# An attention and two-MLP kernel that pins every engine's instruction order with its own list schedule

## Chip, cores and metric

One core of a Trainium2 chip. The metric is device microseconds of one execution, the median of several runs. The profile is of one execution; times in it count from the span's start.

## What is computed

```python
# attention: batch 4, heads 8, seq 576, head_dim 64; f is a forget gate
scores = scale * (q @ k^T) + cum[:, :, :, None] - cum[:, :, None, :]   # cum = cumsum(log(clip(f)))
scores = where(causal, -1e9, scores)
x = softmax(scores) @ v                     # reshaped to 2304 tokens x 512
# first MLP, d_ff 2048
h = x @ w_in
g = h * tanh(softplus(h))
x = g @ w_out
# second MLP, d_ff 1024
h = x @ w_in2
solu = h * softmax(h)
ln = (solu - mean) / sqrt(var + 1e-6) * g_ln
out = ln @ w_out2
```

The weights of the MLPs arrive as 64-bit floats; every product is made of three products of 16-bit halves (high and low).

## The kernel before

The kernel is one stream of instructions that `emit` writes in program order. A scheduler of the framework then sets each engine's order by its own estimate of when operands are there; the kernel adds order edges by hand (`later`) in a few places. Engines run in order and wait on semaphores.

**Head.** SP loads k, q, v in chunks of 128 rows. `split_k`, `split_q`, `split_v` scale a chunk and split it into halves (`split`, L198 to L206: a cast on ScalarE, a subtraction on VectorE or GpSimd); DMA transposes bring k and q into place (L376, L398). The first MLP's weights come in 16 parts of 1 MB (`wi_r0` to `wi_r7`, `wo_r0` to `wo_r7`, two buffers), loaded at L124. `Weight.conv` turns a part into 32-bit floats with three VectorE instructions (L137, L139, L141) and squares it on TensorE into a Gram matrix (L160); after every second part `Weight.bound` finds a scale and `Weight.split` splits the two parts.

**Attention.** For each batch b, row block i (0 to 4) and group of heads: scores on TensorE (L436 to L441), maximum on VectorE (L483, L496), exponential on ScalarE (L485, L499, L500), high half by one of three engines (L519 GpSimd, L521 VectorE, L523 ScalarE), low half by GpSimd (L524), a DMA transpose (L529), and three pv-matmuls per chunk (L555 to L557). `fin` scales the result (L570 to L574) and transposes it into `xT`.

**First MLP.** 9 blocks of 256 tokens, 16 column tiles each. `up` makes a tile of h with 12 matmuls (L785). For two tiles at a time, `mish_a` and `mish_b` compute the activation (ScalarE L797 to L805, VectorE's clamp L802 on `ta` and its product L806 on `th`), `mish_c` casts and subtracts (ScalarE L811, GpSimd L812), and `down` adds the tile into the block's outputs (L829, 12 matmuls for two tiles and each half). Block 0 is accumulated in four parts on VectorE (L838, L840). `evac` scales the block's rows (L851 to L871) and stores them.

**Second MLP.** Its weights (`w2i_r0` to 3, `w2o_r0` to 3) are loaded when attention's memory is released, converted and scaled in the same way (squares on ScalarE, L150; row scale L147; sum over partitions on TensorE, L984). `first` computes 24 matmuls per token tile into h2 (L1028), the normalised z on VectorE, ScalarE and GpSimd (L1035 to L1056), and transposes it; `second` does the last 24 matmuls (L1068).

Program order interleaves these: `att_slots` says how many attention steps go ahead of each half tile of the first MLP, `wgo` how many weight steps.

Of the kernel before, what the change touches and what calls it, by code (L numbers as in the profile page):

```python
# [2 lines left out]

# [19 lines left out]
DFF, DFF2 = 2048, 1024  # L23
NC1 = DM // P
# [62 lines left out]
def later(tc, a, b):

    tc.add_manual_dep(
        getattr(a, "ins", a), getattr(b, "ins", b).name,  # L90
        mybir.DependencyInfo(mybir.DependencyClass.NoSync, mybir.DependencyReason.DATA),
        reason="issue order")
# [9 lines left out]
class Weight:  # L102

    last = None

    def __init__(self, tc, pool, nm, dst, slots, src, across, group=None, row_scale=None, after=None, gram=None):
        self.across = across  # L110
        self.tc, self.nc, self.pool, self.nm, self.dst, self.n = tc, tc.nc, pool, nm, dst, slots // 2
        self.src, self.row_scale = src, row_scale
        self.group, self.after, self.gram = (group or slots) // 2, after, gram
        self.f64 = src(0).dtype != F32
        self.f32 = dst.rearrange("p s e -> p (s e)").bitcast(F32).rearrange("p (s e) -> p s e", e=512)
        if gram is None:
            self.stat = pool.tile([P, self.n], F32, name=f"{nm}_stat")
        self.raw, self.scale, self.slot = {}, {}, {}
        self.bounds = pool.tile([P, self.n // self.group, 8], F32, name=f"{nm}_b")

    def load(self, n):
        src = self.src(n)
        t = self.pool.tile([P, 2, 512], src.dtype, tag="w64", name=f"{self.nm}_r{n}", bufs=WB)
        i = self.nc.sync.dma_start(t, src)  # L124
        if self.after is not None and self.after():
            later(self.tc, i, self.after())
        self.raw[n] = t
        return i

    def conv(self, n):  # L130
        nc = self.nc
        raw = self.raw.pop(n)
        f = self.f32[:, 2 * n + 2:2 * n + 4]
        if self.f64:
# [18 lines left out]
        g, r = divmod(n, self.group)  # L153
        if r == 0:
            self.slot[g] = self.gram.pop(0)
            self.gram.append(self.slot[g])
        o = self.slot[g]
        w = f.bitcast(BF16).rearrange("p s (c e t) -> p (s c) e t", c=4, t=2)[:, :, :, 1]
        for c in range(8):
            i = nc.tensor.matmul(  # L160
                o, w[:, c], w[:, c], start=(r == 0 and c == 0), stop=(r == self.group - 1 and c == 7))
            if c == 0 and Weight.last is not None:
                later(self.tc, i, Weight.last)
            Weight.last = i
# [44 lines left out]
def emit(tc, q, k, v, f, w_in, w_out, w2_in, w2_out, g_ln, out):  # L209
    nc = tc.nc  # L210
# [10 lines left out]
        out=maskd, in_=maskd, pattern=[[-1, P]], compare_op=ALU.is_ge,  # L221
# [19 lines left out]
    win = const.tile([P, NC1 * DFF // 512 + 2, 1024], F16, name="win")  # L241
# [17 lines left out]
    ft = rp0.tile([B * H, S], F32, name="ft")  # L259
    nc.sync.dma_start(ft, f.rearrange("b h s -> (b h) s"))  # L260
    nc.vector.tensor_scalar(ft, ft, 1e-4, 1.0, op0=ALU.max, op1=ALU.min)
    lf = rp0.tile([B * H, S], F32, name="lf")
    first_ln = nc.scalar.activation(lf, ft, AF.Ln)
    with tc.issue_after(getattr(first_ln, "ins", first_ln)):
        nc.scalar.preload_act_table_set("natural_log_exp_and_others")
    nc.vector.memset(ft, 1.0)
    dt_ = rp0.tile([B * H, S], F32, name="dt_")
    nc.vector.tensor_tensor_scan(dt_, ft, lf, 0.0, op0=ALU.mult, op1=ALU.subtract)
# [19 lines left out]
    kt, vt, qt = {}, {}, {}  # L288
# [102 lines left out]
    def split_q(b, c):  # L391
        r0, r1_, t0 = rows_of(b, c)
        t = attd.tile([P, H, P], F16, tag="qn", name=f"qn_{b}_{c}", bufs=1)
        rq = hd(raw["q", b, c][r0:r1_])
        s = sc["q", b][r0:r1_]
        split(nc, t[r0:r1_, :, :64], t[r0:r1_, :, 64:], rq, s, qmode(b, c, 2))
        qa = attd.tile([P, H, P], F16, tag="qa", name=f"qa_{b}_{c}", bufs=2)
        pend["qt"] = nc.sync.dma_start_transpose(out=qa[:, :, r0:r1_], in_=t[r0:r1_].rearrange("p h d -> p (h d)"))  # L398
        qb_ = qb[cnt["qb"] % 2]
        cnt["qb"] += 1  # L400
        nc.vector.tensor_copy(qb_[:64, :, r0:r1_], qa[:64, :, r0:r1_])  # L401
        qt[b, c] = (qa, qb_)

    pend = {}
# [97 lines left out]
    def step_h(b, i, hs):  # L502
        m, pt = pend.pop(("p", b, i, hs))
        n = len(hs) * (i + 1)
# [20 lines left out]
        if n == i + 1 and o == 0:  # L525
            pend["ph", b, i] = ph
            return
        pT = attd.tile([P, 4 * NCH, P], F16, tag="pT", name=f"pT_{b}_{i}_{h0}", bufs=PTB)
        pend["pt"] = nc.sync.dma_start_transpose(  # L529
            out=pT[:, :2 * (o + n), :m], in_=ph[:m, :2 * (o + n)].rearrange("p c s -> p (c s)"))  # L530
        pend["pT", b, i, h0] = pT

# [26 lines left out]
    def fin(b, i):  # L559
# [168 lines left out]
    def pool0(c):  # L728
        return spare if c < 3 else None
# [390 lines left out]
```

## Time and profile before

| | |
|---|---|
| three runs, us | 857.27, 857.79, 859.59 (median 857.79) |
| span of the profiled execution, us | 856.0 |
| TensorE busy | 739.0 us (86%) |
| VectorE busy | 617.6 us (72%) |
| ScalarE busy | 548.2 us (64%) |
| GpSimd busy | 440.8 us (51%) |
| mean granted TensorE clock | 0.977 |
| HBM read, written | 46.59 MB, 9.55 MB |

Which execution was profiled is not among the numbers, so its own time is its span plus what lies outside it; the median of the runs is 1.8 us above the span. Busy time counts an instruction from start to end, so it holds the time in which an instruction has begun and waits inside. Matmuls overlap, and a busy TensorE is not one at its full pace.

### The profile page before, as it was taken

To read this page: it belongs to the slowest core of one execution; us is meant where nothing else is said; L and a number is where in the kernel's file an instruction comes from. 1 tells how busy PE (TensorE), PEld (TensorE's weight loads), DVE (VectorE), ACT (ScalarE), POOL (GpSimd) and SP (SyncE) were. 2 spreads that over 40 slices of the span, in tenths; PEclk is the share of its full clock that TensorE was granted. 3 is DMA by queue.
4 is the path that set the end of the run, shared out by engine and by line. 5 is a ranking of instruction groups with operands and counts; after the bars stand their busy time and mean duration, and the time that the engine had idled before them with its cause. 6 is when DMAs were issued, how large, how long until landed. Compare 5 with 4: busy or idle time off the path is not lost.

```text
span 856.0 us, 15746 instructions
## 1 busy us (share of the span) xinstructions
PE 739.0 (86%) x5822; PEld 456.4 (53%) x5822; DVE 617.6 (72%) x1158; ACT 548.2 (64%) x1202; POOL 440.8 (51%) x341
## 2 busy tenths in 40 slices
PE   0545776689999999997999999986999999999998
PEld 0334543447656666575666767553555554444443
DVE  6799999498867989769896755599566444665551
ACT  5645647868779877877877767686855554333331
POOL 2268676755976667755678653128832222022110
PEclk9999997889999999999999999999999999999999
DMA  9999555477899898988897533941013323344443
GB/s 239 229 215 281 160 176 94 93 137 145 153 174 190 168 169 153 184 155 153 173 180 119 115 70 63 233 156 61 26 38 87 74 64 73 87 101 106 104 88 82
DMA packets 328568, 114.83 MB, mean 134 GB/s; under 512 B 317676, under 2 KB 317676, under 8 KB 328492
## 3 DMA queue, kind: packets, MB, share of 16 engines
q1 hardware_dynamic: 328492, 113.84, 63.9%
q8 instruction: 45, 0.74, 0.4%
q14 instruction: 31, 0.25, 0.1%
HBM read 46.59 MB, written 9.55 MB: 66 GB/s over the span
## 4 chain that ended last, share of the span: by engine, by line
PE 37%; DVE 24%; DMA 12%; ACT 11%; issue 8%; POOL 6%; SPq 1%; DVEq 0%; ACTq 0%; POOLq 0%
PE h L1028 11%; PE o L1068 10%; PE x L829 7%; PE h L785 6%; DMA pT<-ph 3%; POOL ph L524 3%; DVE th L806 2%; DVE ta L802 2%; ACT p L485 2%; DVE ph L521 1%; DMA w2i_r<-in_moe_w_in_dram 1%; DMA ktr<-kn 1%; DMA rawk<-in_k_dram 1%; ACT p L500 1%; DVE nm L483 1%
## 5 line engine op out<-in xcount | busy, mean ns | idle before, releaser
L829 PE MATMUL x<-wout,gt 128*128 128x512 f16 x864 | 219.8, 387 | 18.2 <-ACT gt L811 8.8
L785 PE MATMUL h<-xT,win 128*128 128x256 f16 x1728 | 221.2, 277 | 2.3 <-POOL win L203 1.7
L524 POOL TENSOR_TENSOR ph<-p,ph 128x512 f16<-128x512 f32 (+4 forms) x120 | 157.0, 1314 | 81.3 <-ACT ph L523 35.0
L785 PEld LDWEIGHTS <-win 128*128 128x128 f16 x1728 | 168.5, 100 | 45.8 <-POOL win L203 1.8
L812 POOL TENSOR_TENSOR gt<-th,gt 128x512 f16<-128x512 f32 x72 | 92.4, 1284 | 106.5 <-ACT gt L811 105.3
L829 PEld LDWEIGHTS <-gt 128*128 128x128 f16 x864 | 80.0, 100 | 99.3 <-ACT gt L811 11.6
L1056 POOL TENSOR_TENSOR z<-sl,z 128x1024 f16<-128x1024 f32 x18 | 38.7, 2151 | 138.0 <-DVE s2c L1035 111.1
L1028 PE MATMUL h<-w,x2T 128*128 128x512 f16 x432 | 98.4, 380 | 2.9 <-POOL w L206 1.6
L1068 PE MATMUL o<-wo,zT 128*128 128x512 f16 x432 | 96.5, 379 | 0.5 <-DMA zT<-z 0.5
L555 PE MATMUL pv<-vt,pT 128*128 128x64 f16 (+3 forms) x480 | 71.4, 203 | 23.0 <-DMA pT<-ph 20.2
L806 DVE SCALAR_TENSOR_TENSOR th<-ta,th 128x512 f32<-128x512 f32 x72 | 71.9, 1000 | 24.7 <-ACT ta L805 24.4
L485 ACT ACTIVATE p<-sp,nm 64x64 f32<-64x64 f32 (+7 forms) x128 | 61.3, 484 | 38.7 <-DVE nm L483 21.1
L436 PE MATMUL sp<-ktr,qa 128*128 128x64 f16 (+6 forms) x304 | 59.6, 253 | 22.8 <-ACT p L485 8.7
L811 ACT CAST gt<-th 128x512 f16<-128x512 f32 x72 | 44.3, 615 | 50.2 <-DVE th L806 49.9
L802 DVE TENSOR_SCALAR ta<-ta 128x512 f32<-128x512 f32 x72 | 58.8, 816 | 20.4 <-ACT ta L797 19.9
L1028 PEld LDWEIGHTS <-x2T 128*128 128x128 f16 x432 | 42.3, 98 | 53.9 <-issue 4.0
L555 PEld LDWEIGHTS <-pT 128*128 128x128 f16 (+3 forms) x480 | 45.4, 101 | 47.9 <-DMA pT<-ph 31.3
L556 PE MATMUL pv<-vt,pT 128*128 128x64 f16 (+3 forms) x480 | 70.4, 198 | 0.6 <-DVE vt L199 0.6
L557 PE MATMUL pv<-vt,pT 128*128 128x64 f16 (+3 forms) x480 | 70.2, 198 | 0.0
L1068 PEld LDWEIGHTS <-zT 128*128 128x128 f16 x432 | 42.2, 98 | 51.5 <-DMA zT<-z 1.0
L437 PE MATMUL sp<-ktr,qb 67*128 67x64 f16 (+6 forms) x304 | 63.3, 254 | 3.6 <-DVE qb L401 3.6
L1039 ACT ACTIVATE e<-h,s2c 128x1024 f32<-128x1024 f32 x18 | 21.7, 1204 | 68.1 <-DVE s2c L1037 68.1
(235 smaller groups left out, 1443.5 us busy)
## 6 DMA issues: line engine op xcount, KB each, us to landing
wi_r<-in_moe_w_in_dram SPq DMA_DIRECT2D x8, 1024.0 KB
wo_r<-in_moe_w_out_dram SPq DMA_DIRECT2D x8, 1024.0 KB
rawk<-in_k_dram SPq DMA_DIRECT2D x25, 256.0 KB
rawv<-in_v_dram SPq DMA_DIRECT2D x25, 256.0 KB
x2d<-x2h SPq DMA_DIRECT2D x18, 256.0 KB
out_dram<-ro SPq DMA_DIRECT2D x18, 256.0 KB
w2i_r<-in_moe_w_in_dram SPq DMA_DIRECT2D x4, 1024.0 KB
w2o_r<-in_moe_w_out_dram SPq DMA_DIRECT2D x4, 1024.0 KB
```

Source lines behind the costliest of these rows:

```text
L485: nc.scalar.activation(pv[:m, g * (i + 1) * P + off:g * (i + 1) * P + end], s3[:, g, off:end], AF.Exp, bias=nm[:m, g:g + 1], accum_out=rs[ ...
L524: nc.gpsimd.tensor_tensor(p4[:, :, 1], pv3, p4[:, :, 0], op=ALU.subtract)
L555: nc.tensor.matmul(o, pT[a0:a1, k, :m], vh, start=(c == 0), stop=False)
L556: nc.tensor.matmul(o, pT[a0:a1, k, :m], vl, start=False, stop=False)
L557: nc.tensor.matmul(o, pT[a0:a1, k + 1, :m], vh, start=False, stop=(c == i))
L785: nc.tensor.matmul(ph, win[:, (fi // 4) * NC1 + c, col:col + P], x[:, lx * NC1 + c, :], start=(m == 0), stop=(m == 3 * NC1 - 1))
L802: nc.vector.tensor_scalar(ta, ta, E20, 1.0, op0=ALU.min, op1=ALU.add)
L806: nc.vector.scalar_tensor_tensor(th, ta, 2.5, th, op0=ALU.subtract, op1=ALU.mult)
L812: nc.gpsimd.tensor_tensor(gt[:, 1], th, gt[:, 0], op=ALU.subtract)
L829: nc.tensor.matmul(o, gt[:, lg, n % 2, t * P:(t + 1) * P], wout[:, fi, lw * 512:(lw + 1) * 512], start=(first and m == 0), stop=(last and ...
L1028: nc.tensor.matmul(h[:, half * 512:(half + 1) * 512], x[:, lx * NC1 + c, :], self.w2[:, half * NC1 + c, lw * 512:(lw + 1) * 512], start=(n ...
L1068: nc.tensor.matmul(o, zT[:, lz * NF2 + c, :], self.wo[:, c, lw * 512:(lw + 1) * 512], start=(n == 0), stop=(n == 3 * NF2 - 1))
```

## The change

All order edges written by hand go (`later`, `Weight.last`, `after=`, `issue_after`). At the end of `emit` a new class `Order` reads the whole list of instructions, works out which depends on which (operands, buffers that rotate, pools that are released), gives each a duration from a formula, and runs a list schedule: at each moment the ready instruction that stands first in program order goes to its free engine. VectorE and GpSimd instructions that use the port shared by the two hold a lock. TensorE has a model of its clock, SP one of the DMA queue's backlog. The order that comes out on each engine is pinned by an order edge from each instruction to the next. Instructions, tiles and the program order of `emit` stay.

```diff
-class Weight: ... last = None; ... later(self.tc, i, Weight.last)
...
+EARLY = {"PE": 0.0, "ACT": 103.0, "DVE": 79.0, "POOL": 37.0, "SP": -45.0}
+LATE = {"PE": 53.0, "ACT": 34.0, "DVE": 33.0, "POOL": 77.0, "SP": 27.0}
+HEAD = 126.0
[...]
+BACKLOG = 1500.0
+LANDED = 600.0
...
+        if eng == "POOL":
+            if kind == "InstTensorTensor":
+                return 175 + 1.905 * n, True
+            return 185 + 0.835 * n, True
...
+        if kind == "InstTensorTensor" or len(ins) - len(cols) > 1:
+            return 135 + 1.07 * n + (50 if len(ins) > 2 else 0), len(ins) > 1
...
+                if e in ("DVE", "POOL") and state["lock"] - HEAD > t + 1e-9:
+                    x = min((x for x in ready[e] if not ops[x[1]].lock), default=None)
+                elif e == "SP" and state["dma"] - t > BACKLOG:
+                    x = None
+                else:
+                    x = ready[e][0]
...
+            elif o.lock:
+                end = seen = max(t + HEAD, state["lock"]) + max(o.d - HEAD, 20.0)
+                state["lock"] = end - 8
...
+    def pin(self):
+        seq = self.plan([o.k for o in self.ops])
+        info = mybir.DependencyInfo(mybir.DependencyClass.NoSync, mybir.DependencyReason.DATA)
+        for e in ENGS:
+            row = [i for o in seq[e] for i, _ in o.ins]
+            for a, b in zip(row, row[1:]):
+                self.tc.add_manual_dep(b, a.name, info, reason="order")
```

In the changed kernel the lines have other numbers: L137, L139, L141 are L123, L125, L127; L199 is L182; L802 and L806 are L781 and L785; L124 is L113; L302 is L284; L376, L378 are L358, L360; L398 is L380; L529 is L511; L177 is L160; L147 is L133; L175 is L158.

Every engine's order moves. Three places follow. First VectorE in the head, where the first MLP's weights are converted (`wi_r`, `wo_r` are raw parts, `ta`, `th` tiles of the first MLP's block 0). Before:

```order
L139 SCALAR_TENSOR_TENSOR win<-wi_r_589,win 128x1024
L175 TENSOR_REDUCE wo_b<-gram 128x1
L141 SCALAR_TENSOR_TENSOR win<-wi_r_589,win 128x1024
L802 TENSOR_SCALAR ta_825<-ta_825 128x512
L177 TENSOR_SCALAR wo_b<-sum 128x1
...
L139 SCALAR_TENSOR_TENSOR win<-wi_r_612,win 128x1024
L806 SCALAR_TENSOR_TENSOR th_826<-ta_825,th_826 128x512
L141 SCALAR_TENSOR_TENSOR win<-wi_r_612,win 128x1024
L802 TENSOR_SCALAR ta_1030<-ta_1030 128x512
```

Now:

```order
L127 SCALAR_TENSOR_TENSOR win<-wi_r_589,win 128x1024
L123 TENSOR_SCALAR win<-wi_r_612 128x1024
L125 SCALAR_TENSOR_TENSOR win<-wi_r_612,win 128x1024
...
L127 SCALAR_TENSOR_TENSOR win<-wi_r_612,win 128x1024
L123 TENSOR_SCALAR wout<-wo_r_648 128x1024
L781 TENSOR_SCALAR ta_825<-ta_825 128x512
L125 SCALAR_TENSOR_TENSOR wout<-wo_r_648,wout 128x1024
L158 TENSOR_REDUCE wi_b<-gram 128x1
L127 SCALAR_TENSOR_TENSOR wout<-wo_r_648,wout 128x1024
```

The first pair of `ta` and `th` moved behind later conversions; ahead of the last conversion stand five pairs before and one now, and `wo_r0`'s conversion, which stood among the first score maxima, moved behind the first two v-splits.

Second SP in the head, round the transposition of q's chunk (0,3). Before:

```order
L124 DMA wi_r2_344<-in_moe_w_in_dram 128x2x512
L398 DMA_TRANSPOSE qa_0_2_423<-qn_0_2_419 128x8x128
L529 DMA_TRANSPOSE pT_0_1_0_354<-ph_0_1_0_351 128x8x128
L302 DMA rawk_1_0_837<-in_k_dram 64x8x64
L302 DMA rawv_1_0_839<-in_v_dram 64x8x64
L529 DMA_TRANSPOSE pT_0_1_2_406<-ph_0_1_2_403 128x8x128
L398 DMA_TRANSPOSE qa_0_3_790<-qn_0_3_786 128x8x128
```

Now:

```order
L113 DMA wo_r4_648<-in_moe_w_out_dram 128x2x512
L284 DMA rawq_0_3_676<-in_q_dram 128x8x64
L284 DMA rawk_1_0_837<-in_k_dram 64x8x64
L358 DMA_TRANSPOSE ktr_124<-kn0_125 128x8x64
L113 DMA wo_r5_689<-in_moe_w_out_dram 128x2x512
L113 DMA wi_r6_745<-in_moe_w_in_dram 128x2x512
L380 DMA_TRANSPOSE qa_0_3_790<-qn_0_3_786 128x8x128
```

The load of chunk (0,3), its transposition and the loads of batch 1 moved behind weight loads up to `wi_r6`.

Third VectorE at the second-stage weights (`w2i_r`, `w2o_r` raw parts, `wo` and `w` the converted weights). Before:

```order
L137 TENSOR_SCALAR wo2_6996<-w2o_r0_7355 128x1024
L172 TENSOR_REDUCE w2i_b_7014<-w2i_stat_7013 128x1
L139 SCALAR_TENSOR_TENSOR wo2_6996<-w2o_r0_7355,wo2_6996 128x1024
L802 TENSOR_SCALAR ta_55_7435<-ta_55_7435 128x512
L141 SCALAR_TENSOR_TENSOR wo2_6996<-w2o_r0_7355,wo2_6996 128x1024
L147 TENSOR_SCALAR wo2_6996<-wo2_6996,gl_7008 128x512 x2
L806 SCALAR_TENSOR_TENSOR th_54_7379<-ta_54_7378,th_54_7379 128x512
```

Now:

```order
L127 SCALAR_TENSOR_TENSOR w2_6995<-w2i_r3_7269,w2_6995 128x1024
L781 TENSOR_SCALAR ta_55_7435<-ta_55_7435 128x512
L781 TENSOR_SCALAR ta_56_7494<-ta_56_7494 128x512
L155 TENSOR_REDUCE w2i_b_7014<-w2i_stat_7013 128x1
L123 TENSOR_SCALAR wo2_6996<-w2o_r0_7355 128x1024
L125 SCALAR_TENSOR_TENSOR wo2_6996<-w2o_r0_7355,wo2_6996 128x1024
```

`ta_55` and `ta_56` moved ahead of the first `w2o` conversion, and `th_54` ahead of all these rows. On TensorE the sum for `w2o` (L984) moved back past 96 up-matmuls, 76 down-matmuls and 34 h2-matmuls.

## Rows read from the trace of the kernel before

**Rows 1.** The page, busy time of each engine, share of the span, instructions.

```profile
PE 739.0 (86%) x5822; PEld 456.4 (53%) x5822; DVE 617.6 (72%) x1158; ACT 548.2 (64%) x1202; POOL 440.8 (51%) x341
```

**Rows 2.** By stage: PE, PEld, DVE, ACT, POOL busy, granted clock, DMA share, GB/s.

```profile
0.00:140.50 140.50, 76.43 (x578) 51.77 (x578) 125.60 (x192) 80.05 (x166) 79.62 (x54) 0.95 0.84 201
140.50:200.00 59.50, 45.40 (x432) 29.17 (x431) 43.48 (x99) 47.41 (x112) 39.95 (x30) 0.86 0.67 131
200.00:537.00 337.00, 315.63 (x3201) 217.80 (x3200) 261.39 (x467) 261.92 (x637) 226.16 (x203) 0.99 0.81 147
537.00:606.00 69.00, 55.78 (x360) 34.93 (x359) 55.94 (x83) 51.51 (x89) 30.96 (x19) 0.98 0.48 142
606.00:856.00 250.00, 245.79 (x1260) 122.74 (x1257) 131.19 (x320) 107.35 (x203) 64.08 (x38) 1.00 0.35 78
...
50.00:150.00 100.00, 67.58 (x496) 43.30 (x493) 96.21 (x143) 58.32 (x110) 74.89 (x42) 0.91 0.73 181
```

**Rows 3.** The chain, 640 to 690 us: start us, us, what.

```profile
661.10 1.31 PE h L785 x12
662.41 1.29 PE x L829 x6
```

**Rows 4.** TensorE's groups, 200 to 550 us: count, busy us, mean ns, idle before.

```profile
L785 PE MATMUL h<-xT,win 128*128 128x256 f16 x1032 | 132.8, 274 | 0.0
L829 PE MATMUL x<-wout,gt 128*128 128x512 f16 x528 | 132.5, 380 | 6.0 <-ACT gt L811 3.5 <-POOL gt L812 1.6 <-DVE x2h L858 0.8
```

**Rows 5.** Single lines, whole span: duration ns min/median/max, first and last start.

```profile
L802 DVE TENSOR_SCALAR ta<-ta x72: 367/798/2343, 87.8 to 717.7; 128x512 f32<-128x512 f32 x72
L806 DVE SCALAR_TENSOR_TENSOR th<-ta,th x72: 631/692/3330, 92.6 to 720.2; 128x512 f32<-128x512 f32 x72
L139 DVE SCALAR_TENSOR_TENSOR win<-wi_r,win x8: 1205/1226/3019, 15.4 to 121.0; 128x1024 int32<-128x1024 int32 x8
L812 POOL TENSOR_TENSOR gt<-th,gt x72: 1147/1158/2137, 97.6 to 723.3; 128x512 f16<-128x512 f32 x72
```

**Rows 6.** The timeline at 215 and 337 us: start us, us, instruction.

```profile
214.84 1.31 POOL L812 TENSOR_TENSOR gt<-th,gt 128x512 f16<-128x512 f32 x1
215.47 0.97 DVE L802 TENSOR_SCALAR ta<-ta 128x512 f32<-128x512 f32 x1
...
337.04 1.16 POOL L812 TENSOR_TENSOR gt<-th,gt 128x512 f16<-128x512 f32 x1
337.19 1.02 DVE L871 SCALAR_TENSOR_TENSOR us<-x2m,kb 64x1 f32<-64x1 f32 x1
```

**Rows 7.** VectorE's groups by shape, 0 to 200 us.

```profile
L139 DVE SCALAR_TENSOR_TENSOR win<-wi_r,win 128x1024 int32<-128x1024 int32 x8 | 13.4, 1681 | 0.1
L141 DVE SCALAR_TENSOR_TENSOR wout<-wo_r,wout 128x1024 int32<-128x1024 int32 x8 | 13.3, 1663 | 0.0
...
L802 DVE TENSOR_SCALAR ta<-ta 128x512 f32<-128x512 f32 x10 | 8.8, 881 | 0.0
...
L806 DVE SCALAR_TENSOR_TENSOR th<-ta,th 128x512 f32<-128x512 f32 x9 | 7.8, 870 | 0.0
...
L840 DVE SCALAR_TENSOR_TENSOR acc<-x,rho,acc 128x512 f32<-128x512 f32 x6 | 4.4, 743 | 1.4 <-PE x L829 1.4
```

**Rows 8.** TensorE's groups, 0 to 140.5 us.

```profile
L785 PE MATMUL h<-xT,win 128*128 128x256 f16 x144 | 20.4, 302 | 1.7 <-POOL win L203 1.7
L829 PE MATMUL x<-wout,gt 128*128 128x512 f16 x60 | 16.4, 419 | 2.0 <-POOL gt L812 1.0 <-ACT gt L811 0.8
```

**Rows 9.** VectorE's timeline: first conversions of wo parts, and the last one.

```profile
25.52 0.68 DVE L137 TENSOR_SCALAR wout<-wo_r 128x1024 int32<-128x1024 int32 x1
...
44.02 0.68 DVE L137 TENSOR_SCALAR wout<-wo_r 128x1024 int32<-128x1024 int32 x1
...
138.68 1.21 DVE L141 SCALAR_TENSOR_TENSOR wout<-wo_r,wout 128x1024 int32<-128x1024 int32 x1
```

**Rows 10.** Who waited for whom, 200 to 480 us: us, times, longest.

```profile
POOL ph L524 <- DVE ph L521: 25.5, 18, 4.9
...
ACT gt L811 <- DVE th L806: 15.7, 12, 2.9
```

**Rows 11.** Second-stage weights: the chain, TensorE's timeline, TensorE's groups 537 to 606 us.

```profile
537.05 6.71 DMA w2i_r<-in_moe_w_in_dram
...
599.22 0.38 PE L984 MATMUL sum<-w2o_b,ones 128*128 128x1 f32 x2 [1.07 <-DVE w2o_b L172]
...
L829 PE MATMUL x<-wout,gt 128*128 128x512 f16 x112 | 28.2, 392 | 9.3 <-ACT gt L811 4.4 <-DVE x2h L858 3.8 <-POOL gt L812 1.0
```

More of the change, by code (lines that the diff above doesn't have):

```diff
@@ L1 @@
+import heapq
 import math
@@ L84, in part_of @@
     return w[c * P:(c + 2) * P, fr * 512:(fr + 1) * 512].rearrange("(s p) e -> p s e", p=P)
[L87 to L92, printed above, removed]
 def root2(nc, dst, x):
@@ L102, with __init__ @@
 class Weight:
-    last = None
-    def __init__(self, tc, pool, nm, dst, slots, src, across, group=None, row_scale=None, after=None, gram=None):
+    def __init__(self, tc, pool, nm, dst, slots, src, across, group=None, row_scale=None, gram=None):
         self.across = across
@@ L112, in __init__ @@
         self.src, self.row_scale = src, row_scale
-        self.group, self.after, self.gram = (group or slots) // 2, after, gram
+        self.group, self.gram = (group or slots) // 2, gram
         self.f64 = src(0).dtype != F32
@@ L123, in load @@
         t = self.pool.tile([P, 2, 512], src.dtype, tag="w64", name=f"{self.nm}_r{n}", bufs=WB)
-        i = self.nc.sync.dma_start(t, src)
-        if self.after is not None and self.after():
-            later(self.tc, i, self.after())
+        self.nc.sync.dma_start(t, src)
         self.raw[n] = t
-        return i
     def conv(self, n):
@@ L159, in conv @@
         for c in range(8):
-            i = nc.tensor.matmul(
+            nc.tensor.matmul(
                 o, w[:, c], w[:, c], start=(r == 0 and c == 0), stop=(r == self.group - 1 and c == 7))
-            if c == 0 and Weight.last is not None:
-                later(self.tc, i, Weight.last)
-            Weight.last = i
     def bound(self, g):
@@ L262, in emit @@
     lf = rp0.tile([B * H, S], F32, name="lf")
-    first_ln = nc.scalar.activation(lf, ft, AF.Ln)
-    with tc.issue_after(getattr(first_ln, "ins", first_ln)):
-        nc.scalar.preload_act_table_set("natural_log_exp_and_others")
+    nc.scalar.activation(lf, ft, AF.Ln)
+    nc.scalar.preload_act_table_set("natural_log_exp_and_others")
     nc.vector.memset(ft, 1.0)
@@ L397, in split_q @@
         qa = attd.tile([P, H, P], F16, tag="qa", name=f"qa_{b}_{c}", bufs=2)
-        pend["qt"] = nc.sync.dma_start_transpose(out=qa[:, :, r0:r1_], in_=t[r0:r1_].rearrange("p h d -> p (h d)"))
+        nc.sync.dma_start_transpose(out=qa[:, :, r0:r1_], in_=t[r0:r1_].rearrange("p h d -> p (h d)"))
         qb_ = qb[cnt["qb"] % 2]
@@ L528, in step_h @@
         pT = attd.tile([P, 4 * NCH, P], F16, tag="pT", name=f"pT_{b}_{i}_{h0}", bufs=PTB)
-        pend["pt"] = nc.sync.dma_start_transpose(
+        nc.sync.dma_start_transpose(
             out=pT[:, :2 * (o + n), :m], in_=ph[:m, :2 * (o + n)].rearrange("p c s -> p (c s)"))
@@ L596, in emit @@
     grams = [gram[:, n * P:(n + 1) * P] for n in range(4)]
-    Weight.last = None
     attd = ea.enter_context(tc.tile_pool(name="attd", bufs=1, side="right"))
@@ L601, in emit @@
     W1 = Weight(
-        tc, wst, "wi", win, NC1 * DFF // 512, lambda n: part_of(w_in, n), across, group=4,
-        after=lambda: pend.get("pt"), gram=grams)
+        tc, wst, "wi", win, NC1 * DFF // 512, lambda n: part_of(w_in, n), across, group=4, gram=grams)
     W2 = Weight(
         tc, wst, "wo", wout, NF1, lambda n: part_of(w_out, n), across,
-        group=4, after=lambda: pend.get("pt"), gram=grams)
+        group=4, gram=grams)
     usc_done = set()
@@ L743, in emit @@
         split_q(0, c)
-    first = pend["qt"]
     for c in range(1, NCH):
-        later(tc, load_raw(0, c, "v", pool0(c)), first)
-    later(tc, load_raw(0, 2, "q", pool0(2)), first)
+        load_raw(0, c, "v", pool0(c))
+    load_raw(0, 2, "q", pool0(2))
     wgo(W0C)
@@ L958, in emit, with __init__ @@
     st2.rest()
+    Order(tc).pin()
     es.close()
+class Op:
+    def __init__(self, k, eng):
+        self.k, self.eng = k, eng
+        self.ins, self.deps, self.od, self.succ, self.osucc = [], set(), set(), [], []
+        self.d, self.lock, self.cols, self.span, self.first = 0.0, False, 0.0, 0.0, 0.0
+ENGS = ("PE", "ACT", "POOL", "DVE", "SP")
+ENG_OF = {"PE": "PE", "Activation": "ACT", "Pool": "POOL", "DVE": "DVE", "SP": "SP"}
+EARLY = {"PE": 0.0, "ACT": 103.0, "DVE": 79.0, "POOL": 37.0, "SP": -45.0}
```

289 lines of the change are left out of this document (added).

## The prediction

> **What bounds the kernel now.** I read the page first: TensorE is busy 739.0 of 856.0 us, more than any other engine [rows 1]. The table by stage says where the other 117 us are [rows 2]. Up to 140.5 us TensorE is busy 76.4 us, in the next 59.5 us 45.4 us, from 200 to 537 us 315.6 of 337 us, in the 69 us in which the second-stage weights are prepared 55.8 us, and from 606 us to the end 245.8 of 250 us. So the last 250 us belong to TensorE: no order makes them shorter, and what is won must be won ahead of 606 us, as an earlier start of that saturated stretch.
>
> Busy time flatters TensorE. In the chain of the saturated stretch 12 up-matmuls take 1.31 us and 6 down-matmuls 1.29 us, or 0.109 and 0.216 us each [rows 3]. Between 200 and 550 us 1032 of the one and 528 of the other are in flight for 132.8 and 132.5 us [rows 4], where at that pace they need 112.5 and 114.0. So up to 39 us stand there beside the open idle time of 21.4 us.
>
> What holds TensorE ahead of 606 us is what feeds it: VectorE busy 96.2 and GpSimd 74.9 of the 100 us from 50 to 150 us [rows 2]. That is partly waiting. The clamp L802 takes 0.367 us at best, 0.798 us in the median and 2.343 us at worst for one shape, and L806 0.631 to 3.330 us; a conversion instruction L139 goes from 1.205 to 3.019 us [rows 5]. The timeline shows why: an L802 that begins at 215.47 us, while GpSimd's L812 runs (214.84 to 216.15), lasts 0.97 us and ends 0.29 us after it; an L871 one element wide lasts 1.02 us and ends with the L812 beside it [rows 6]. Instructions that get in each other's way like this are what the change's planner treats as one resource (`lock`, and `HEAD`, 126 ns, in its code).
>
> The Trainium skill, SBUF — State Buffer, section "SBUF: two separate sides", calls the shared pair an exclusive lock, held by whichever comes first for its whole instruction, the other fully blocked. The trace agrees that the loser waits, but the L802 above, 0.37 us long at its shortest, ends 0.29 us after the L812, so some 0.08 us of it ran beside. By the page's rule each change of owner would cost that 0.08 us more, an order would have less to win in the head, and term A below would be near nothing: 836 us by this sum.
>
> **The change part by part.** No instruction's work changes. Removed are the `later` edges; added is an order for each engine. So I cost three stretches by what moved.
>
> *A, the head (to 200 us).* In both orders the same 144 pv-matmuls and 84 score-matmuls stand ahead of the last Gram matmul. Ahead of it stand now 24 up- and 12 down-matmuls, where the trace has 144 and 60 [rows 8]: block 0 of the first MLP is put behind the weight conversions. That is 120 x 0.109 + 48 x 0.216 = 23.5 us of TensorE work later than before. What it buys is an earlier end of the conversions. Before, wo_r1's conversion begins at 44.0 us and the last L141 ends at 139.9 us [rows 9], 95.9 us for 13 parts. Now 14 parts stand behind the first two v-splits: 3.1 us more (0.68 + 2 x 1.21). Four ta/th pairs leave that stretch, 4 x (0.88 + 0.87) = 7.0 us, and four accumulator instructions of about 0.74 us, 3.0 us. Four GpSimd subtractions L812 go with them, 4 x 1.16 = 4.6 us less to wait for [rows 5, 7]. Of the waits in the L139 and L141, (1.67 - 1.21) x 28 = 12.9 us [rows 7], I give half to the better order, 6.5 us. That leaves 95.9 + 3.1 - 7.0 - 3.0 - 4.6 - 6.5 = 78 us, an end near 122 us. From there to 200 us, at the share of the middle stretch (0.94 busy, full clock), TensorE does 73 us; less the 23.5 us in arrears that is 49.8 us. Before, 45.4 us at a granted clock of 0.86 (a mixture of the levels 1.2 and 2.4 GHz) are worth 39.0 us from 140.5 to 200 us. **Term A: -10 us** (-10.8, rounded down). Ends: conversions done at 110 us give -22; at 143 us (95.9 + 3.1, no relief) +9. I take the value for 122 us since the instructions that left are counted and only the half is a choice.
>
> On SP the transposition of q chunk (0,3) and the loads of batch 1 move behind wi and wo loads. I cost this at nothing: attention block (0,3) resumes in both orders only at the end of the conversions. If a weight load stalls there, those rows stall with it (second rival).
>
> *B, the middle (200 to 537 us).* The order of TensorE's blocks stays nearly the same. What can go is waiting: open idle 21.4 us and up to 39 us of thin flow. The table of waits names the links that reach TensorE: GpSimd's L524 behind VectorE's copy 25.5 us, the cast behind L806 15.7 us [rows 10]. Lower bound -40 us (two thirds of 60: ScalarE is busy 261.9 of 337 us, so not all can go), upper bound +10 us (half the open idle again, if the planned durations miss and engines wait in the pinned order). **Term B: -12 us**, a fifth of the slack, nearer to the small end, because waits on VectorE and GpSimd are mostly off TensorE's path at 94% busy.
>
> *C, the second-stage weights (537 to 606 us).* Before, the first w2 load starts at 537.05 us, and TensorE's sum for w2o starts at 599.22 us; TensorE idles 13.2 us in the stretch, 9.3 us of it ahead of down-matmuls [rows 11]. In the new order, ahead of that w2o sum, stand 96 up-, 76 down- and 34 h2-matmuls more: 10.5 + 16.4 + 7.3 = 34.2 us of work that no longer waits for it, because VectorE now does ta and th between w2o's steps. Late next is the split of w2 on GpSimd, ahead of the first h2. **Term C: -10 us**, ends -13 and 0.
>
> *The tail* stays: the same z chain ends it, and TensorE is full. 0 us.
>
> *Sum:* 856.0 - 10 - 12 - 10 = 824.0 us of span. The median of the three runs is 857.8, 1.8 us above the profiled span; I add that: **825.8 us**. All lower ends give 781 + 1.8, all upper ends 875 + 1.8.
>
> **Rivals.**
> 1. *More than that:* once conversions end early and waits fall in the middle, thin flow fills and B reaches -40: 856 - 10 - 40 - 10 + 1.8 = 798 us. For it: 60 us of slack. Against it: ScalarE at 78% and attention's chain of transposes.
> 2. *Slower: late weights.* If wo_r0's conversion, moved from 25.5 us [rows 9] to behind the v-splits, delays everything, and SP's in-order queue holds buffers, the conversions end at 143 us or later, with 23.5 us of MLP still owed. At the middle's pace the head then loses 9 us, at the pace seen from 140.5 to 200 us (39.0 of 59.5) it does 37 us by 200 us, owes 23.5 and is 25 us behind. Midway 17 us, with B and C nothing: 856 + 17 + 1.8 = 875 us. It decides at the end of the last L127 on wout: by 139 us or later than that.
> 3. *No change: the resource is full already.* From 50 to 150 us VectorE and GpSimd together show 171 us of busy time in 100 us. If nearly all is work on the shared resource, no order shortens it, and A and B are nothing; C is then paid for by h2 arriving late: 856 to 858. Against it: the medians far above the shortest [rows 5]. [...]
>
> **How the numbers follow.** A measurement of this kernel tells about 0.3% (2.6 us) from no change. The forecast's case (806 to 846 us) gets 0.61; the first rival 0.15; the second 0.14; the third 0.10, of which 0.06 lie within 0.3%, 0.02 on either side. Faster: 0.61 + 0.15 + 0.02 = 0.78; same 0.06; slower 0.14 + 0.02 = 0.16. The range 798 to 862 us takes in the forecast, the first rival's value and the third, and leaves out most of the second and what lies below 798 us. The forecast's own range is 806 to 846 us.
>
> **What would show it.** Right: the last conversion ends near 122 us with block 0 of the MLP hardly begun; the median of L802 between 200 and 537 us falls from 0.8 us towards 0.4; TensorE idles under 5 us between the first w2 load and the w2o sum; the last 250 us look as before, 30 us earlier. Wrong: conversions that end after 139 us; L802 as slow as before; or a saturated stretch that begins at 606 us all the same.

## The result, and the profile after

The changed kernel takes 845.67 us in the median (845.53 to 847.40, four runs) against 858.69 us (857.27 to 860.99, four runs) for the kernel before beside it: a ratio of 0.9845, 95% interval 0.9825 to 0.9865. It is faster, by 13 us where 32 were forecast. The profiled execution has a span of 843.7 us.

The page of the changed kernel, busy time; to be read beside [rows 1]:

```profile
PE 734.2 (87%) x5822; PEld 456.5 (54%) x5822; DVE 598.6 (71%) x1158; ACT 544.6 (65%) x1201; POOL 440.6 (52%) x341
```

The same stretches as in [rows 2], after (PE, PEld, DVE, ACT, POOL busy, granted clock, DMA share, GB/s):

```profile
0.00:140.50 140.50, 53.43 (x402) 36.87 (x402) 114.65 (x179) 63.98 (x138) 79.27 (x55) 0.82 0.84 201
140.50:200.00 59.50, 55.01 (x484) 36.30 (x484) 38.80 (x85) 51.88 (x116) 30.87 (x24) 0.94 0.55 106
200.00:537.00 337.00, 327.00 (x3329) 226.65 (x3329) 257.23 (x495) 270.87 (x663) 234.15 (x208) 0.99 0.85 152
537.00:606.00 69.00, 65.03 (x422) 40.61 (x421) 59.09 (x83) 53.38 (x92) 31.28 (x20) 1.00 0.45 141
50.00:150.00 100.00, 47.24 (x372) 32.91 (x373) 85.96 (x131) 38.61 (x71) 66.75 (x37) 0.73 0.76 194
...
593.70:843.70 250.00, 245.90 (x1257) 122.52 (x1255) 140.67 (x340) 112.80 (x209) 69.26 (x39) 1.00 0.38 83
```

The middle and the second-stage weights went as forecast: from 200 to 537 us TensorE is busy 327.0 us instead of 315.6, from 537 to 606 us 65.0 instead of 55.8. The last 250 us do what they did, 245.9 us against 245.8, and begin 12 us earlier. The head is where the two pictures part: up to 140.5 us TensorE does 53.4 us instead of 76.4, as forecast, but the conversions that were to end early do not.

VectorE's timeline at the end of the conversions, and GpSimd's beside it (start, duration):

```profile
131.63 3.03 DVE L127 SCALAR_TENSOR_TENSOR wout<-wo_r,wout 128x1024 int32<-128x1024 int32 x1
...
136.14 3.02 DVE L125 SCALAR_TENSOR_TENSOR wout<-wo_r,wout 128x1024 int32<-128x1024 int32 x1
139.20 2.06 DVE L127 SCALAR_TENSOR_TENSOR wout<-wo_r,wout 128x1024 int32<-128x1024 int32 x1
```

```profile
135.65 2.44 POOL L189 TENSOR_TENSOR win<-win 128x1024 f16<-128x1024 f32 x1
```

The last L127 ends at 141.3 us; the last L141 ended at 139.9 [rows 9]. The conversion of 136.14 us takes 3.02 us where 1.21 is the shortest: it ends 1.07 us after the L189 that it meets (135.65 + 2.44 = 138.09). So the port is met in the planned order too. The groups of the conversions up to 200 us, after (count, busy us, mean ns, idle before):

```profile
L125 DVE SCALAR_TENSOR_TENSOR wout<-wo_r,wout 128x1024 int32<-128x1024 int32 x8 | 14.9, 1864 | 0.1
L127 DVE SCALAR_TENSOR_TENSOR wout<-wo_r,wout 128x1024 int32<-128x1024 int32 x8 | 14.4, 1804 | 0.1
L125 DVE SCALAR_TENSOR_TENSOR win<-wi_r,win 128x1024 int32<-128x1024 int32 x8 | 13.6, 1695 | 0.1
L127 DVE SCALAR_TENSOR_TENSOR win<-wi_r,win 128x1024 int32<-128x1024 int32 x8 | 10.5, 1309 | 0.1
```

Together 53.4 us for 32 instructions, 1.67 us each, the same mean as before [rows 7]. What VectorE waits for between 50 and 141 us, after:

```profile
DVE wo_b L160 <- PE sp L311: 1.9, 1, 1.9
DVE win L123 <- DMA wi_r<-in_moe_w_in_dram: 1.9, 1, 1.9
DVE nm L465 <- PE sp L423: 1.3, 2, 0.7
DVE wo_b L158 <- PE gram L146: 1.3, 2, 0.7
DVE wi_b L158 <- PE gram L146: 1.1, 1, 1.1
DVE wi_b L160 <- PE sum L311: 0.7, 1, 0.7
DVE wi_b L160 <- PE sp L311: 0.7, 1, 0.7
```

With the smaller ones these are 10.2 us; before, the same table held three waits of 1.9 us in all. Seven tenths of it is waiting for TensorE, and TensorE in turn waits for VectorE. Its waits for conversions between 84 and 150 us, after, then before:

```profile
PE gram L146 <- DVE wout L127: 18.7, 5, 8.4
PE gram L146 <- DVE win L127: 13.1, 3, 6.6
```

```profile
PE gram L160 <- DVE win L141: 3.7, 2, 3.2
...
PE gram L160 <- DVE wout L141: 1.8, 2, 1.6
```

The two engines work in turns: a conversion, its Gram matmuls, its sums, the next scale. TensorE stands idle for conversions in 31.8 us, where it was 5.5; block 0 of the MLP, which it did meanwhile before, is put behind.

### The profile page after: what moved, and what is told of

Same layout as the page of the kernel before. It is cut to its first block, busy times and chain, and to the rows that moved or that the text cites. A ratio compares the mean times of both kernels' runs of the same rounds, so it can differ in the third digit from the quotient of the medians.

```text
span 843.7 us, 15751 instructions
## 1 busy us (share of the span) xinstructions
PE 734.2 (87%) x5822; PEld 456.5 (54%) x5822; DVE 598.6 (71%) x1158; ACT 544.6 (65%) x1201; POOL 440.6 (52%) x341
## 4 chain that ended last, share of the span: by engine, by line
PE 53%; DVE 16%; ACT 10%; DMA 10%; issue 5%; POOL 5%; SPq 1%; POOLq 0%; DVEq 0%; ACTq 0%
PE x L808 14%; PE h L764 12%; PE h L1371 9%; PE o L1411 7%; PE pv L537 3%; DMA pT<-ph 2%; PE sp L418 2%; PE sp L419 2%; DMA rawk<-in_k_dram 2%; DMA w2i_r<-in_moe_w_in_dram 2%; POOL ph L506 1%; DMA rawv<-in_v_dram 1%; ACT p L467 1%; DVE wout L127 1%; POOL gt L791 1%
## 5 line engine op out<-in xcount | busy, mean ns | idle before, releaser
L808 PE MATMUL x<-wout,gt 128*128 128x512 f16 x864 | 213.9, 385 | 9.9 <-POOL gt L791 6.0
L764 PE MATMUL h<-xT,win 128*128 128x256 f16 x1728 | 209.9, 275 | 1.4 <-ACT th L777 1.4
L506 POOL TENSOR_TENSOR ph<-p,ph 128x512 f16<-128x512 f32 (+4 forms) x120 | 159.7, 1338 | 55.3 <-ACT ph L505 34.0
L791 POOL TENSOR_TENSOR gt<-th,gt 128x512 f16<-128x512 f32 x72 | 91.3, 1270 | 101.7 <-ACT gt L790 101.6
L1371 PE MATMUL h<-w,x2T 128*128 128x512 f16 x432 | 96.0, 379 | 0.1
L537 PE MATMUL pv<-vt,pT 128*128 128x64 f16 (+3 forms) x480 | 71.6, 202 | 12.7 <-DMA pT<-ph 12.6
L785 DVE SCALAR_TENSOR_TENSOR th<-ta,th 128x512 f32<-128x512 f32 x72 | 58.7, 817 | 23.4 <-ACT ta L784 20.4
L418 PE MATMUL sp<-ktr,qa 128*128 128x64 f16 (+6 forms) x304 | 58.6, 255 | 15.4 <-ACT p L467 13.1
L465 DVE TENSOR_REDUCE nm<-sp 128x1 f32<-128x320 f32 (+7 forms) x88 | 48.5, 562 | 22.4 <-PE sp L423 11.9
L776 ACT ACTIVATE ta<-h,usc 128x512 f32<-128x512 f32 (+3 forms) x96 | 53.7, 576 | 14.3 <-PE h L764 14.2
```

The source lines that it names most:

```text
L418: nc.tensor.matmul(d, qa[:, h, r0:r1_], k1, start=True, stop=False)
L506: nc.gpsimd.tensor_tensor(p4[:, :, 1], pv3, p4[:, :, 0], op=ALU.subtract)
L537: nc.tensor.matmul(o, pT[a0:a1, k, :m], vh, start=(c == 0), stop=False)
L764: nc.tensor.matmul(ph, win[:, (fi // 4) * NC1 + c, col:col + P], x[:, lx * NC1 + c, :], start=(m == 0), stop=(m == 3 * NC1 - 1))
L791: nc.gpsimd.tensor_tensor(gt[:, 1], th, gt[:, 0], op=ALU.subtract)
L808: nc.tensor.matmul(o, gt[:, lg, n % 2, t * P:(t + 1) * P], wout[:, fi, lw * 512:(lw + 1) * 512], start=(first and m == 0), stop=(last and ...
```

## The experiments

To compare orders I read from each trace when TensorE had done the same work: the recorded matmuls in order of time, each counted as its columns at 2.4 GHz (27 ns at least). The table gives how far a run is behind (+) or ahead (-) of the kernel before at equal work; in the kernel before the six points lie at 101.6, 199.3, 346.8, 539.4, 594.9 and 839.6 us. Each row is read from one profiled execution; the runs that leave the head's order to the framework differ among themselves by several us already at 80 us of columns. The step to the second column is the head, from there to the fourth the middle (B), to the fifth the second-stage weights (C), and the last is the second stage.

| run | 25 | 80 | 200 | 360 | 400 | 640 us of columns | median us | ratio, 95% |
|---|---|---|---|---|---|---|---|---|
| the change | +41.1 | +11.3 | +4.1 | -1.5 | -12.7 | -11.9 | 845.67 | 0.9825 to 0.9865 |
| e1 head alone | +40.1 | +11.6 | +13.0 | +15.5 | +14.2 | +15.0 | 871.88 | 1.0132 to 1.0170 |
| e2 middle alone | +1.6 | +3.4 | -3.9 | -9.7 | -10.8 | -7.9 | 850.82 | 0.9879 to 0.9931 |
| e3 second stage alone | -0.2 | -1.0 | -0.8 | -0.3 | -12.8 | -12.0 | 847.05 | 0.9845 to 0.9886 |
| e4 middle, second stage | +1.1 | +2.0 | -4.4 | -11.9 | -21.8 | -21.0 | 836.38 | 0.9729 to 0.9768 |
| e5 gram outside rotation | +17.7 | +8.4 | +1.2 | -3.2 | -15.6 | -15.7 | 840.85 | 0.9759 to 0.9797 |
| e6 change, no port | +42.8 | +12.4 | +19.6 | +17.6 | +17.2 | +24.8 | 881.97 | 1.0244 to 1.0276 |
| e7 = e4, no port | +2.3 | +5.5 | +11.4 | +10.7 | +9.7 | +18.4 | 876.65 | 1.0183 to 1.0222 |
| e8 = e5, 100 places | +5.1 | +4.1 | +3.2 | -5.3 | -17.2 | -17.2 | 840.42 | 0.9767 to 0.9812 |
| e9 = e5, 200 places | -9.1 | -0.5 | -2.0 | -10.3 | -21.6 | -20.5 | 838.11 | 0.9743 to 0.9787 |
| e10 = e5, 400 places | -9.6 | +3.8 | -0.2 | -8.2 | -18.3 | -17.6 | 838.45 | 0.9735 to 0.9788 |

### One stage at a time: e1 to e4

The planner plans everything, but only the instructions of some stages get order edges; the others are left to the framework, the head then with its `later` edges. An instruction belongs to the stage in which `emit` writes it: the head until block 1's first up-matmul (`hn == 2 * NF1`), the middle until `Stage2` is built.

```diff
+PIN = "MT"
...
-    Order(tc).pin()
+    Order(tc, cuts).pin()
...
+            o.stage = "HMT"[sum(n >= c for c in self.cuts)]
...
-            row = [i for o in seq[e] for i, _ in o.ins]
+            row = [o for o in seq[e] if o.stage in PIN]
+            row = [i for o in row for i, _ in o.ins]
```

The head alone, `PIN = "H"`. Expected:

> Order edges only for what is issued before block 1's first-MLP matrices (the head: loads, weights, attention of the first slots, block 0); the framework schedules the rest. The trace after the change has the head's conversions end at 140.4 us (139.9 before) and TensorE 11 us behind at equal matmul columns by 205 us. Theory 1 (the head's order costs some 11 us that nothing later gives back by itself; the middle's order is worth 12 of its own, the second stage's 11): about 869 us, 11 over the kernel before. Theory 2 (the deferred work only fills slack of the middle, and the middle's gain is nothing but that catching up): 856 to 860 us.

Measured: 871.88 us, 13.7 over the 858.17 of the kernel before, as theory 1 has it. The 11.6 us lost in the head are not taken up by the framework's middle; it adds 4 more.

The middle alone, `PIN = "M"`. Expected:

> Order edges only for what is issued from block 1 on until the second stage's weights begin; head and second stage by the framework, with the edges that the kernel before had. Theory 1: the middle's order is worth its 12 to 13 us alone, 845 to 848 us, and the median clamp (TENSOR_SCALAR ta) falls from 0.80 to about 0.42 us. Theory 2: without a deferred backlog there is nothing to catch up, 856 to 860 us, though the clamp's median falls just as far.

Measured: 850.82 us, -7.3: 2.8 us above theory 1's range and 5.2 below theory 2's. The table says what is missing: the middle itself gains 13.1 us (from +3.4 to -9.7), but 3.4 are lost ahead of it and 2.9 in the second stage, in the framework's order. The clamp falls as expected, to a median of 0.426 us over the whole run. There was no backlog here to catch up, so the middle's gain is its own.

The second stage alone, `PIN = "T"`. Expected:

> Order edges only for the second stage and its weights. Both theories: the stretch in which TensorE waits for the second-stage weights (537 to 606 us before) gives back 10 to 12 us, so 846 to 849 us; a third view, that those weights come in time only because the middle is ordered too, gives 856 to 860 us.

Measured: 847.05 us, -11.1. Term C stands by itself, with the framework's order in the middle as with the planner's. The stretch from 537 to 606 us in e3:

```profile
537.00:606.00 69.00, 65.72 (x432) 41.72 (x430) 59.75 (x81) 54.18 (x95) 30.67 (x20) 1.00 0.46 141
```

TensorE is busy 65.7 of 69 us, where it was 55.8 [rows 2].

Both, without the head, `PIN = "MT"`. Expected:

> Order edges for the middle and the second stage, the head as in the kernel before. Theory 1: -12 and -11 without the head's +11, so 833 to 837 us, faster than both kernels. Theory 2: the backlog is gone and so is its catching up, 845 to 848 us, as with all three.

Measured: 836.38 us, -21.8: theory 1, and faster than both kernels by more than their intervals. So the head's order costs the change some 9 us (845.67 less 836.38; their ratios to the kernel before differ by 0.0097, or 8 us), and without it term B and term C add up.

### Why the head costs: e5

The planner takes tiles with the same tag to rotate: the third tile needs all uses of the first to be over.

```python
q = tags.setdefault((tag, str(t._space)), [])
q.append(nm)
...
if bufs and len(q) > bufs:
    rotated.append((len(ops), q[-1 - bufs], i))
```

In PSUM the tag `h` has two buffers, and the first tile with it is `gram`, which lives until the last conversion. Block 0's second h tile is the third of that tag. So its matmuls are planned behind the last Gram matmul. The kernel needs nothing of the kind: before, that h tile and four more ran ahead of the last Gram matmul [rows 8]. In e5 `gram` stands outside the rotation, and block 0's h tiles count on the one buffer that is left.

```diff
-                        if tag:
+                        if tag and not nm.startswith("gram"):
...
+                            if nm.startswith("h_0_"):
+                                bufs = 1
```

> All three stages ordered as in the change, with one thing mended in the planner's picture of PSUM: the change takes block 0's second h tile (the third tile with the tag h, whose pool has two buffers) to need the buffer of the gram tile, which is in use until the last conversion, and so plans it behind that conversion; here gram stands outside the rotation and block 0's h tiles count on one buffer. Theory 1a (this false dependence is what deferred block 0 and made the head cost): the second h tile's matmuls start near 90 us instead of 141, the granted clock between 75 and 150 us rises from 0.57-0.73 to 0.8 or more, and the time is 833 to 840 us. Theory 1b (block 0 was deferred for other reasons, or the deferring isn't what costs): 844 to 848 us, as the change itself.

Measured: 840.85 us, just above what theory 1a gives and well below 1b. Block 0's up-matmuls in e5, TensorE's timeline:

```profile
96.86 2.72 PE L792 MATMUL h<-xT,win 128*128 128x256 f16 x12 [4.86 <-ACT th L805]
...
106.86 5.28 PE L792 MATMUL h<-xT,win 128*128 128x256 f16 x24 [3.75 <-ACT th L805]
...
149.19 2.77 PE L792 MATMUL h<-xT,win 128*128 128x256 f16 x12
```

The second h tile starts at 96.9 us instead of 142.1, the third at 106.9, and the fourth only after the conversions, at 149.2. So the false dependence is a part of the head's price, 4.8 us by the medians (5.8 by the ratios to the kernel before), and something else still holds block 0 back. The granted clock, expected at 0.8 or more, rose only in part: 0.76 from 100 to 125 us, where the change has 0.57, but 0.70 in the 25 us before that and 0.58 in the 25 us after.

### What still holds it: e8, e9, e10

Among the instructions that are ready the planner takes the one that stands first in program order. The third h tile's scale, a one-element instruction on VectorE (`usc`), stands in the program behind the last conversion, and so it waited there behind all of them (in e5 it runs at 144.8 us). In e8 to e10 block 0's MLP instructions are given a priority some places ahead of their own.

```diff
+EAGER = 200
...
+    def block0(self, o):
+        return o.stage == "H" and o.eng != "SP" and any(
+            w and t.name.startswith(("h_0_", "ta_", "th_", "gt_", "x2_0_", "usc1", "acc"))
+            for _, acc in o.ins for t, b, w in acc)
...
-        seq = self.plan([o.k for o in self.ops])
+        seq = self.plan([o.k - EAGER * self.block0(o) for o in self.ops])
```

With 100 places:

> As the run with gram outside the rotation, and in the planner's priority (the place in program order) block 0's MLP operations in the head stand 100 places further ahead, so that a one-element scale on VectorE that is ready no longer queues behind the conversions that were written earlier. Theory 2a (what the head still costs, some 5 us against the head of the kernel before, is this priority): block 0's third to eighth h tiles run before the conversions end, the granted clock between 125 and 150 us rises from 0.58 to 0.8 or more, the time is 831 to 837 us. Theory 2b (VectorE has no room: what block 0 takes, the conversions lose): the last conversion ends 5 us or more after 141 us and the time is 840 to 846 us.

Measured: 840.42 us, no better than e5, and at the lower edge of 2b's window. The last conversion does not come later (139.8 us), so 2b's reason is not seen. Of 2a the clock nearly came (0.77 from 125 to 150 us), and five h tiles run before the conversions end, where e5 has three and 2a wanted eight; the time did not come. At 45 us of columns e8 is some 19 us behind the kernel before; it makes up most of that by 80.

With 200 places:

> The same with 200 places. Theory 2a: as with 100 places or a little better, 830 to 837 us. Theory 2b: conversions later still, 842 to 850 us.

Measured: 838.11 us, a little above 2a's window and below 2b's. TensorE is level with the kernel before at 80 us of columns (-0.5), and the conversions end sooner than in any other run. VectorE's timeline in e9:

```profile
128.29 3.02 DVE L144 SCALAR_TENSOR_TENSOR wout<-wo_r,wout 128x1024 int32<-128x1024 int32 x1
131.24 1.40 DVE L848 SCALAR_TENSOR_TENSOR acc<-x,rho,acc 128x512 f32<-128x512 f32 x2
132.56 2.95 DVE L146 SCALAR_TENSOR_TENSOR wout<-wo_r,wout 128x1024 int32<-128x1024 int32 x1
```

The last one ends at 135.5 us, with 12 of block 0's `ta`, `th` and `acc` instructions on VectorE ahead of it where the change has two. So it was not block 0's work on VectorE that kept the conversions at 140 us. TensorE from 75 to 150 us, first in the change, then in e9 (columns as above):

```profile
75.00:100.00 25.00, 8.53 (x76) 6.61 (x76) 23.56 (x25) 6.92 (x9) 11.50 (x7) 0.73 0.64 173
100.00:125.00 25.00, 10.42 (x54) 5.96 (x54) 20.63 (x34) 10.74 (x20) 18.73 (x9) 0.57 0.93 244
125.00:150.00 25.00, 14.72 (x125) 10.79 (x123) 20.57 (x34) 10.46 (x19) 18.70 (x11) 0.61 0.49 114
```

```profile
75.00:100.00 25.00, 20.28 (x168) 14.82 (x167) 23.76 (x29) 13.65 (x21) 14.29 (x7) 1.00 0.47 159
100.00:125.00 25.00, 14.48 (x94) 8.49 (x92) 23.39 (x36) 8.56 (x12) 18.32 (x9) 0.68 0.56 174
125.00:150.00 25.00, 15.49 (x90) 8.72 (x89) 21.71 (x37) 17.16 (x29) 14.76 (x10) 0.78 0.34 81
```

With 400 places:

> The same with 400 places. Theory 2a (the head's price was a matter of priority alone, and 200 places have paid it back): TensorE is ahead of the kernel before or level with it at 200 us, as with 200 places, and the time stays at 834 to 839 us. Theory 2b (with more, the conversions are what comes too late): the last conversion ends after 141 us, and the time goes up again to 841 us or more.

Measured: 838.45 us, inside 2a's window, though the last conversion ends at 146.5 us, as 2b expected. So here the two effects pull against each other: TensorE is 9.6 us ahead at 25 us of columns and 3.8 behind at 80. Between 200 and 400 places the time is flat. The two corrections together win back most of the head's price; e4, with the head as it was, and e9 can't be told apart by their intervals. Of the two, the first is clear of noise; the 2.7 us from e5 to e9 are not, since those intervals overlap too.

### What the port is worth: e6 and e7

The planner keeps its durations, and lets VectorE and GpSimd overlap freely.

```diff
-                o.d, o.lock = self.duration(o.eng, *o.ins[0])
+                o.d = self.duration(o.eng, *o.ins[0])[0]
```

On the change itself:

> The change with the port taken out of the plan: VectorE's and GpSimd's instructions keep their durations, but the planner lets them overlap freely. Theory A (the planned port is what makes the middle's order better): the clamp's median in the middle goes back from 0.42 towards 0.80 us and the middle's 10 to 12 us are lost, 853 to 860 us. Theory B (the list schedule in program order with measured durations is worth it, whatever it knows of the port): the clamp's median rises too, but the time stays at 843 to 849 us.

Measured: 881.97 us, beyond what either theory gave: 2.6% slower than the kernel before. The clamp's median from 200 to 537 us is 0.73 us, as both expected. On e4:

> Middle and second stage ordered, head as before, port taken out of the plan. Theory A: the second stage's 11 us stay, the middle's 10 are lost, 845 to 849 us. Theory B: 834 to 839 us, as with the port in the plan.

Measured: 876.65 us, 40 us above e4 and slower than the kernel before. Theory A has the right sign, and its size was too small: without the port the middle does not fall back to the framework's, it falls below it. The stretch from 200 to 537 us, first in e4, then in e7 (columns as above):

```profile
200.00:537.00 337.00, 325.68 (x3290) 225.09 (x3288) 258.17 (x491) 269.68 (x653) 231.48 (x205) 1.00 0.85 156
```

```profile
200.00:537.00 337.00, 313.21 (x3148) 215.12 (x3147) 259.19 (x469) 259.86 (x629) 226.28 (x202) 0.98 0.82 149
```

And the group of the clamps (`ta`) in that stretch, again e4 and e7:

```profile
L809 DVE TENSOR_SCALAR ta<-ta 128x512 f32<-128x512 f32 x44 | 27.8, 638 | 13.1 <-ACT ta L804 13.1
```

```profile
L809 DVE TENSOR_SCALAR ta<-ta 128x512 f32<-128x512 f32 x40 | 32.4, 813 | 8.9 <-ACT ta L804 8.7
```

The mean of a clamp goes from 0.64 to 0.81 us (0.86 in the kernel before), and TensorE does 12.5 us less in the same time. The links between the engines go back as well (200 to 480 us, e7; in e4 they are 11.1 and 4.4 us, in the kernel before 25.5 and 15.7 [rows 10]):

```profile
POOL ph L531 <- DVE ph L528: 21.0, 13, 4.8
...
ACT gt L818 <- DVE th L813: 12.0, 13, 1.7
```

Yet all three stay below the kernel before, and e7's middle is slower than its middle; what makes up the rest is open. By the table, of the 39 us between e4 and e7 at the end 3.5 lie in the head, whose order is the framework's in both, 19.1 in the middle, 8.9 at the second-stage weights and 7.9 in the second stage. What is lost behind the middle shows in part in TensorE's waits: in e7 from 530 us to the end it waits 9.2 us for VectorE's x2h and 3.7 us for its x2m, in e4 1.0 us for both together. Those rows of e7:

```profile
PE x L836 <- DVE x2h L865: 9.2, 3, 6.3
...
PE h L1408 <- DVE x2m L861: 3.7, 1, 3.7
```

## Why the prediction was right, and where it was wrong

**Term A failed: forecast -10 us, measured +11.** The step that failed is the end of the conversions, "an end near 122 us"; it came at 141.3. The rest of the term held: with 141.3 us, and the granted clock of 0.94 that the trace shows from 140.5 to 200 us, the same sum gives 58.7 us x 0.94 (busy share) x 0.94 (clock) - 23.5 = 28.4 us against 39.0, or +10.6. The sum for the end took 18 us off the 95.9 before: 10.0 for instructions that leave the stretch and 11.1 for waits at the port, less 3.1 for the part added. VectorE's busy time from wo_r1's first conversion to the end of the last one, the same 13 parts, before and after:

```profile
44.02:139.89 95.87, 93.92 (x128) 0.93 0.75 186
```

```profile
45.44:141.26 95.82, 84.35 (x118) 0.73 0.75 195
```

The instructions did leave, and VectorE is busy 9.6 us less; but it stands idle for 11.5 us instead of 2.0, and the stretch is as long as before. The sum had no term for such waits. The relief at the port did not come either: a conversion instruction takes 1.67 us as before. I had treated VectorE as the bound, so that taking work from it must end it sooner. The waits have the look of a ring: TensorE's Gram matmuls wait 31.8 us for conversions, and VectorE waits for Gram and sums; with block 0 behind, nothing fills TensorE's share. That this ring sets the end of the conversions is argued, not shown: where block 0 runs earlier and TensorE's waits for conversions between 84 and 150 us fall, to 8.3, 6.0 and 3.8 us in e8, e9 and e10, the conversions end at 139.8, 135.5 and 146.5 us.

**The deferring itself I took as a purchase.** The text costs it, 23.5 us of TensorE work later, and looks for what it buys. It bought nothing: it came from a false dependence on `gram` (e5) and, by the timelines, from priority by program order (e8 to e10). The rows on the order showed what moved; that the planner's rule on rotating tags was not the program's could have been read in its code.

**Term B was right: forecast -12 us, measured -12.8** (from +11.3 to -1.5), and -13.1 and -13.9 where only the middle, or the middle and the second stage, are ordered. The reason given for it fits: the clamp's median falls from 0.798 us [rows 5] to 0.421 over the whole run and from 0.89 to 0.43 from 200 to 537 us, the two links of [rows 10] from 25.5 and 15.7 us to 9.1 and 5.8, and without the port in the plan the gain turns into a loss. All occurrences of the clamp, then the two links from 200 to 480 us, after:

```profile
L781 DVE TENSOR_SCALAR ta<-ta x72: 367/421/2349, 98.9 to 706.4; 128x512 f32<-128x512 f32 x72
```

```profile
POOL ph L506 <- DVE ph L503: 9.1, 8, 2.8
...
ACT gt L790 <- DVE th L785: 5.8, 7, 2.0
```

The fear that B only fills what A left behind fell with e2.

**Term C was right: forecast -10 us, measured -11.2** (from -1.5 to -12.7), -12.5 alone in e3. The mechanism is the one named: the sum for w2o comes at 621.4 us instead of 599.2 [rows 11], behind work that no longer waits for it, and ahead of it TensorE idles 4.0 us (82.5 less 78.5), where under 5 were forecast. The change from the first w2 load on:

```profile
537.50:606.00 68.50, 64.53 (x420) 40.34 (x419) 58.59 (x83) 52.88 (x91) 31.28 (x20) 1.00 0.45 143
606.00:620.00 14.00, 14.00 (x84) 8.12 (x83) 10.59 (x19) 10.91 (x20) 4.89 (x3) 1.00 0.29 52
```

And TensorE's timeline at the sum:

```profile
621.37 0.28 PE L1327 MATMUL sum<-w2o_b,ones 128*128 128x1 f32 x2
```

**The sum:** 856.0 + 11.3 - 12.8 - 11.2 = 843.3 us against a span of 843.7 us. So all of the miss of 20 us lies in term A, which came out beyond its own upper end (+9). The time lies just inside the forecast's own range (806 to 846 us), which is due to the width of that range and not to its sum.

**The rivals.** The second, late weights, had the right place and sign for the head: its point of decision, an end of the last L127 at 139 us or later, was passed, and the 11 us lie between the 9 and 25 that it gave. Its mechanism, a stall of SP's queue behind wo_r0, was not what happened: from 50 to 141 us VectorE waits for a raw part only once, 1.9 us, and the conversions end 1.4 us later than before, not late. It set B and C to nothing, and they came in full. The third, a resource that is full already, is refuted by e4 and e7: the order on the port decides over 40 us. The first did not come: B ended at a third of its -40.

The Trainium skill, SBUF — State Buffer, section "SBUF: two separate sides", has whichever of the two starts first hold the shared pair for its whole instruction, the other fully blocked. The trace after differs from the page by a little, as the one before did: the L125 of 136.14 us ends 1.07 us after the L189, with 1.21 us as its shortest, so some 0.1 us of it ran beside. The prediction's working of that rule, term A near nothing and 836 us, does not follow from its own figure: 0.08 us more at each of 28 conversion instructions is 2.2 us, not 10.

## What to carry to other kernels

Before you credit an order with what it moves out of a busy engine's way, look whether that engine waits for another that is now idle; where two engines wait for each other, the work taken out can come back as waiting, as 9.6 us did here. A planner's instructions are only as good as its dependences: compare what it puts last with what the old trace ran early, since a buffer rule that is stricter than the program's costs time (here some 5 us). And when one resource is shared by two engines, schedule with it or leave the order to what was there: here the same planner, on the same stages, gains 22 us with it and loses 17 without.

## What was not expected of the hardware

The port's worth: 40 us of 836 (e4 to e7) for a plan that differs only in whether VectorE and GpSimd may overlap, three times what the change gained. The open idle time of TensorE in the middle of the kernel before was 21.4 us, and nothing there pointed to a loss of that size in the other direction.

TensorE's granted clock in the head: in the change it falls to 0.73 of full speed from 75 to 100 us, where the engine is busy 8.5 us, and to 0.57, near the lower level of 1.2 GHz, in the next 25 us; in e9, busy 20.3 us from 75 to 100 us, it stays at 1.00 there. Two rows of TensorE's timeline in the change, eight Gram matmuls each:

```profile
98.41 1.03 PE L146 MATMUL gram<-win 128*128 128x128 bf16 x8 [6.58 <-DVE win L127]
...
120.97 0.62 PE L146 MATMUL gram<-win 128*128 128x128 bf16 x8
```

The same two stretches, with the granted clock behind the busy time:

```profile
98.40:99.45 1.05, 1.03 (x8) 0.50 0.74 107
120.90:121.60 0.70, 0.70 (x11) 1.00 0.95 369
```

Around the first the granted clock is 0.50, the lower level, and they take 1.03 us; around the second it is 1.00, the upper level of 2.4 GHz, and they take 0.62. So in this head a deferred block costs TensorE twice, by its own time and by slower Gram matmuls, for which VectorE waits. How much of the 9 us is the clock was not separated from the waiting.

What bounds the conversions at 135 us in the best order is open. The kernel has buffers for two raw parts; three were not tried.
